# Value rows spread over the partitions, keys written in that order: a block-sparse attention with a gated projection

## The chip, the cores and the metric

The kernel runs on one core of a Trainium2 chip. The metric is the device time of one execution in microseconds, the median of three runs. Engines: TensorE (PE; PEld is its weight load), VectorE (DVE), ScalarE (ACT), GpSimd (POOL) and SyncE (SP), which issues nearly all DMAs.

## The reference

Attention over 4 batches, 8 heads, 768 positions, head size 64. Positions fall into 24 blocks of 32. A query block attends to its own block and both neighbours, to the first and last block, and to three sampled blocks; the first and last query blocks attend to everything. The attention output goes through a gated layer.

```python
mask = np.abs(blk_i - blk_j) <= 1
mask = mask | (blk_i == 0) | (blk_j == 0) | (blk_i == n_blocks - 1) | (blk_j == n_blocks - 1)
for qb in range(n_blocks):
    for kb in sampled_blocks[qb]:
        mask[qb * 32:(qb + 1) * 32, kb * 32:(kb + 1) * 32] = True
scores = np.where(mask, scale * q @ k.T, -1e9)
attn = softmax(scores)                      # rows minus their maximum, exp, divided by the sum
x = (attn @ v)                              # heads side by side: (4, 768, 512)
gate = sigmoid(causal convolution of x with conv_w, 5 taps)
out = (gate * (x @ w_val)) @ w_out
```

## The kernel before

**Places and units.** Batches are taken in two groups of two. Query blocks 1 to 22 form eleven pairs (`PAIRS`); a pair in a group is a *place*, and the list `ORDER` gives their order, with two *global* places (the first and last query block of one batch) put between them, after eight and after nine pairs. A block place gives two *units*, one for each batch of the group; unit 1 and unit 2 of the whole list are exchanged. There are 44 block units.

**One step** of the main loop is: loads for places ahead, `scores` of unit n, key copies for the place ahead, `values` of unit n-2, `transposes` of unit n-1 with up to two pieces of the projection (`fill`, paced by `PACE`) after each half, gate work (`prepare`), and `finish` for the unit whose values are done. Every engine runs its instructions in the program's order (class `InOrder`); the order is fixed when the kernel is built.

**Keys.** `kg` has two buffers, each with 12 slots of one 32-key block: slots 0 to 3 are the first block, the last block and the pair's own two blocks; slots 4 to 7 are the near neighbour and three sampled blocks of the first query block; 8 to 11 the same for the second. Each query block uses slots 0 to 3 and four others, 256 keys. POOL copies them from the resident `keys` (`copy_static`, `copy_sampled`), in the opening partly ACT, and for a few places SP loads the sampled ones from HBM.

**Scores and exponentials.** `scores` fills two PSUM tiles `sc` (heads h = 0, 1) with 32 matmuls; the pool `ps_sc` has three buffers, the third of which the transposed output `xp` takes, so that the next unit's scores use the two tiles that the exponentials read. DVE takes the row maximum of both query blocks (`mx`), and ACT writes four exponentials `pe` of 128 x 256 per unit (two heads, two halves).

**Transposes and values.** PE transposes `pe` in pieces of 128 keys into `pt`, ACT copies them to `ptr`. The key's place among 128 is then its partition, and the values must lie in the same order: `va` holds first, last and own blocks (32 partitions each), `vb` for each query block its near neighbour and three sampled blocks (32 partitions each). The values of a row, two batches with eight heads of 65 numbers, are 4160 bytes.

**Value loads.** `load_values` of a place issues on SP: the end blocks into `va` when the buffer's group changes, the pair's own 64 rows, the near blocks (one DMA for both, or two), a load of six block numbers into registers, and six DMAs of 32 rows each for the sampled blocks. `va` and `vb` have two buffers each; a load waits until PE has used the place before last. For a global place the rows go into 128 partitions.

**The gated layer.** `gates` runs the convolution on DVE with its first tap and tanh on ACT, `split` makes two-part copies of x for exact products (ACT and POOL), `project` does the two products on PE. The weights come as 8-byte integers' worth of double precision and are decoded in the first hundred microseconds: DVE makes `words`, ACT casts to `wv` or `wo`, POOL subtracts for the second part.

Of the kernel before, what the change touches and what calls it, by code (L numbers as in the profile page):

```python
# [11 lines left out]
AF = mybir.ActivationFunctionType  # L12
# [4 lines left out]
B, H, S, D = 4, 8, 768, 64  # L17
BLK, NB, NR = 32, 24, 3
# [47 lines left out]


@with_exitstack
def attention_moe(ctx, tc, qb, kb, v, ve, sampled, w_val, conv_w, w_out, ident_in, slot_in, out):
    nc = tc.nc  # L70
    const = ctx.enter_context(tc.tile_pool(name="const", bufs=1))
    two = ctx.enter_context(tc.tile_pool(name="two", bufs=2))
# [201 lines left out]
    def load_keys(pl):  # L274
        g = pl.gr.g
        if pl.glob:
            return
        pl.kg = kg[pl.kseq % RING]
        if g and pl.p < RING:
            for e in range(EACH):  # L280
                sp.dma_start(pl.kg[:, e, 0:2, :], kb[:, EACH * g + e, 0 : NB : NB - 1, :])
        for place, reg in block_numbers(pl, SP):
            sp.dma_start(
                pl.kg[:, :, place, :],
                kb[:, EACH * g : EACH * g + EACH, bass.ds(reg, 1), :].rearrange("p e o x -> p e (o x)"),
            )
# [8 lines left out]

    def copy_static(pl, e=slice(0, EACH)):
        kt, k, i0 = pl.kg, pl.gr.k, PAIRS[pl.p][0]
        pool.tensor_copy(kt[:, e, 2:4, :], k[:, e, i0 : i0 + 2, :])
        pool.tensor_copy(kt[:, e, 4:9:4, :], k[:, e, i0 - 1 : i0 + 3 : 3, :])
        if pl.p < RING and pl.gr.g == 0:  # L300
            act.copy(kt[:, e, 0:2, :], k[:, e, 0 : NB : NB - 1, :])

    def numbers(pl):
        pl.numbers = {eng: list(block_numbers(pl, eng)) for eng in (POOL, ACT)}
# [15 lines left out]
    def load_values(pl):  # L320
        g = pl.gr.g
        vt = pl.va = va[pl.vseq % VRING]
        pl.vb = two.tile([128, 2, EACH * H * DV], F32, tag="vb", name="vb")
        if pl.glob:
            b = pl.batches[0].b
            x = b % EACH * H * DV
            rows = v[g * S : (g + 1) * S, x : x + H * DV].rearrange("(c p) d -> p c d", p=128)
            vb4 = pl.vb.rearrange("p j (e d) -> p (j e) d", e=EACH)
            for c in range(0, 4, 2):
                sp.dma_start(vb4[:, c : c + 2, :], rows[:, c : c + 2, :])  # L330
            sp.dma_start(vt, rows[:, 4:6, :])
            pl.chunks = [vb4[:, c, :] for c in range(4)] + [vt[:, c, :] for c in range(2)]
            ends.pop(pl.vseq % VRING, None)
            return
        if ends.get(pl.vseq % VRING) != g:
            sp.dma_start(vt[0 : 2 * BLK].rearrange("p e d -> p (e d)"), ve[g])
            ends[pl.vseq % VRING] = g
        i0 = PAIRS[pl.p][0]
        sp.dma_start(
            vt[64:128].rearrange("p e d -> p (e d)"), v[g * S + i0 * BLK : g * S + (i0 + 2) * BLK, :]  # L340
        )
        vblocks = v.rearrange("(n k) d -> n k d", k=BLK)
        if 0 < pl.p < NP - 2:
            sp.dma_start(
                pl.vb[0:BLK], vblocks[g * NB + i0 - 1 : g * NB + i0 + 3 : 3].rearrange("j k d -> k j d")
            )
        else:
            for j, near in enumerate((i0 - 1, i0 + 2)):
                sp.dma_start(pl.vb[0:BLK, j, :], vblocks[g * NB + near if 0 < near < NB - 1 else GROUPS * NB])
        _, regs = nc.values_load_multi_w_load_instructions(  # L350
            sv[0:1, g, i0 : i0 + 2, :].rearrange("p i r -> p (i r)"), engines=[SP], min_val=0, max_val=GROUPS * NB,
            skip_runtime_bounds_check_because="block numbers are drawn from [0, 24)",
        )
        for n, reg in enumerate(regs):
            j, r = n // NR, n % NR
            sp.dma_start(
                pl.vb[BLK * (r + 1) : BLK * (r + 2), j, :], vblocks[bass.ds(reg, 1)].rearrange("o k d -> (o k) d")
            )


# [27 lines left out]
    def scores(un):  # L388
        pr = un.pr
        un.P = []  # L390
        if pr.glob:
            lo = [ps_sc.tile([128, 512], F32, tag="sc", name="s0") for _ in range(2)]
            spaces = ((ps_sc, "sc"), (ps_pt, "pt"))
            hi = [space.tile([128, 512], F32, tag=tag, name="s1") for space, tag in spaces]
            for k0 in range(3):
                for hp, h, rows, cols in heads():
                    dst = hi[h][cols, 0:256] if k0 == 2 else lo[h][cols, 256 * k0 : 256 * k0 + 256]
                    matmul(
                        dst, pr.pl.q[rows, 0, hp, un.e, :], pr.pl.gr.k[rows, pr.i, 8 * k0 : 8 * k0 + 8, cols],
                        start=True, stop=True, tile_position=(64 * h, BLK * hp),  # L400
                    )
            mx = three.tile([128, 2, 4], F32, tag="mx", name="mx")
            rest = five.tile([128, 2, 256], F32, tag="pr", name="rest")
            for h in range(2):
                dve.tensor_reduce(out=mx[:, h, 0:1], in_=lo[h], axis=AX.X, op=ALU.max, negate=True)
                dve.tensor_reduce(out=mx[:, h, 1:2], in_=hi[h][:, 0:256], axis=AX.X, op=ALU.max, negate=True)
                dve.tensor_tensor(out=mx[:, h, 2:3], in0=mx[:, h, 0:1], in1=mx[:, h, 1:2], op=ALU.min)
                first = five.tile([128, 512], F32, tag="pr", name="first")
                act.activation(rest[:, h, :], hi[h][:, 0:256], AF.Exp, bias=mx[:, h, 2:3])
                act.activation(first, lo[h], AF.Exp, bias=mx[:, h, 2:3])  # L410
                un.P.append(first)
            un.P.append(rest.rearrange("p h k -> p (h k)"))
            return
        sc = [ps_sc.tile([128, 2, 256], F32, tag="sc", name="sc") for _ in range(2)]
        kt = pr.pl.kg[:, pr.i].rearrange("p (t e) x -> p t e x", e=4)
        for a in range(2):
            for g in range(4):
                for h in range(2):
                    rows, hp, j = slice(64 * h, 64 * h + 64), 2 * a + g // 2, g % 2
                    matmul(  # L420
                        sc[h][BLK * g : BLK * g + BLK, a, :], pr.pl.q[rows, pr.i, hp, j, :],
                        kt[rows, 0 : 2 + j : 1 + j, :, BLK * hp : BLK * hp + BLK],
                        start=True, stop=True, tile_position=(64 * h, BLK * g),
                    )
        mx = three.tile([128, 2, 4], F32, tag="mx", name="mx")
        for h in range(2):
            dve.tensor_reduce(out=mx[:, h, 0:2], in_=sc[h], axis=AX.X, op=ALU.max, negate=True)
            pe_ = five.tile([128, 2, 256], F32, tag="pr", name="pe")
            for j in range(2):
                act.activation(pe_[:, j, :], sc[h][:, j, :], AF.Exp, bias=mx[:, h, j : j + 1])  # L430
            un.P.append(pe_.rearrange("p j k -> p (j k)"))

    def transposes(un):
# [417 lines left out]
def _layout(inputs):  # L851
    f = np.ascontiguousarray
    k = inputs["k"].reshape(B, HP, 2, NB, BLK, D)
    blocks = np.array([0, NB - 1] + list(range(1, NB - 1)))
    qb = inputs["q"].reshape(B, HP, 2, NB, BLK, D)[:, :, :, blocks].reshape(B, HP, 2, NP, 2, BLK, D)
    qb = f(qb.transpose(2, 6, 0, 3, 1, 4, 5)).reshape(128, B, NP, HP, 2, BLK)
    kb = f(k.transpose(2, 5, 0, 3, 1, 4)).reshape(128, B, NB, HP * BLK)
    vo = np.ones((B, S, H, DV), np.float32)
    vo[..., :D] = inputs["v"].transpose(0, 2, 1, 3)
    vo = vo.reshape(GROUPS, EACH, S, H * DV).transpose(0, 2, 1, 3).reshape(GROUPS * S, EACH * H * DV)  # L860
    vv = np.zeros((GROUPS * S + BLK, EACH * H * DV), np.float32)
    vv[: GROUPS * S] = vo
    ve = f(vo.reshape(GROUPS, NB, BLK, -1)[:, 0 : NB : NB - 1]).reshape(GROUPS, 2 * BLK, EACH * H * DV)
    w_val = f(inputs["moe_w_val"]).view(np.int64)
    w_out = f(inputs["moe_w_out"]).view(np.int64)
    conv = f(inputs["moe_conv_w"].T.reshape(CH, 128, KW).transpose(1, 0, 2)).reshape(128, CH * KW).view(np.int64)
    ident = np.eye(128, dtype=np.float32)
    slot = np.arange(NB, dtype=np.float32)[None]
    return {
        "q": qb, "k": kb, "v": vv, "ve": ve, "sampled": f(np.asarray(inputs["sampled_blocks"], np.int64)),  # L870
        "w_val": w_val, "conv_w": conv, "w_out": w_out, "ident": ident, "slot": slot,
    }

# [20 lines left out]
```

## Time and profile before

| | |
|---|---|
| median of three runs | 393.9 us (393.18 to 394.4) |
| the profiled execution's own time | 396.17 us |
| its span, first to last instruction | 394.4 us |
| PE busy | 345.2 us, 88% |
| DVE busy | 247.0 us, 63% |
| ACT busy | 245.3 us, 62% |
| POOL busy | 155.1 us, 39% |
| DMA, the main queue | 64.03 MB, 58.7% of 16 engines' span |
| mean granted TensorE clock | 0.967 of full |

The shares are averages over stages with different limits: an engine that is busy for 62% of the span can be the bound in one stage and idle in the next. Matmuls are pipelined, so a busy PE is not PE at its peak.

### The profile page before, as it was taken

What the parts mean: (1) busy time and instruction counts of PE and PEld (TensorE: products, weight loads), DVE (VectorE), ACT (ScalarE), POOL (GpSimd) and SP (SyncE); (2) the same over time, 40 slices, a digit from 0 to 9 for tenths busy, and PEclk for the clock granted to TensorE, in tenths of its full rate; (3) what the DMA queues carried; (4) which work ended last, traced back from release to release, by engine and by line L of the source; (5) the groups of instructions that cost most, each with busy time, mean ns of one, the idle gap of its engine ahead of it and who ended that gap; (6) DMA issues with size and microseconds to landing.
All of it is one profiled execution on the core that took longest, in us unless ns stands there. A gap on an engine that the chain in (4) does not pass through costs nothing.

```text
span 394.4 us, 15210 instructions
## 1 busy us (share of the span) xinstructions
PE 345.2 (88%) x6240; PEld 270.1 (68%) x6240; DVE 247.0 (63%) x534; ACT 245.3 (62%) x574; POOL 155.1 (39%) x233
## 2 busy tenths in 40 slices
PE   0589878786999999988899999998999899998985
PEld 0256555564787688856698777866769668887874
DVE  3333777777877873463964895459845665285940
ACT  2665767767678885573766876577746755364531
POOL 1452256647328011325643970327303720344440
PEclk9968999998999999996999999999999989999999
DMA  7996899997625676899865578454345241010202
GB/s 257 282 232 187 238 237 262 264 222 203 179 48 137 238 236 184 265 246 279 233 192 134 129 193 220 103 183 118 109 158 138 64 130 54 2 54 27 75 6 80
DMA packets 34568, 65.08 MB, mean 165 GB/s; under 512 B 4931, under 2 KB 18372, under 8 KB 34500
## 3 DMA queue, kind: packets, MB, share of 16 engines
q1 hardware_dynamic: 34210, 64.03, 58.7%
q8 instruction: 49, 0.80, 0.9%
q14 instruction: 19, 0.16, 0.1%
q10 hardware_dynamic: 290, 0.09, 0.1%
HBM read 57.81 MB, written 6.29 MB: 163 GB/s over the span
## 4 chain that ended last, share of the span: by engine, by line
PE 52%; DVE 17%; issue 9%; DMA 6%; POOL 6%; ACT 4%; SPq 3%; POOLq 1%; ACTq 0%; DVEq 0%
PE vp L87 15%; DVE th L87 10%; PE av L87 9%; PE op L87 9%; PE pt L87 8%; PE sc L87 7%; DVE mx L87 5%; POOL kg L87 4%; DMA vb<-in_v 4%; SPq L87 2%; PE s L87 2%; PE xp L87 2%; DMA keys<-in_k 2%; ACT pe L87 1%; POOLq L251 1%
## 5 line engine op out<-in xcount | busy, mean ns | idle before, releaser
L87 DVE SCALAR_TENSOR_TENSOR th<-xT,cw,th 128x388 f32<-128x388 f32 (+1 forms) x128 | 94.0, 748 | 12.3 <-ACT th L87 9.7
L87 ACT ACTIVATE pe<-sc,mx 128x256 f32<-128x256 f32 x176 | 68.9, 475 | 47.9 <-DVE mx L87 47.8
L87 DVE TENSOR_REDUCE mx<-sc 128x2 f32<-128x512 f32 x88 | 56.5, 683 | 66.5 <-PE sc L87 66.0
L87 POOL COPY kg<-keys 128x256 f32 (+3 forms) x156 | 76.0, 530 | 53.6 <-DMA keys<-in_k 28.1
L87 ACT COPY ptr<-pt 128x512 f32<-128x512 f32 x112 | 64.9, 599 | 25.9 <-PE pt L87 25.7
L87 POOL TENSOR_TENSOR yl<-y,yh 128x384 fp32r<-128x384 f32 x32 | 33.5, 1048 | 118.4 <-ACT yh L87 118.1
L87 PE MATMUL sc<-kg,qc 64*32 64x256 f32 x1408 | 54.7, 397 | 18.3 <-ACT kg L87 10.2
L87 PE MATMUL av<-vb,ptr 128*32 128x65 f32 x1920 | 51.4, 228 | 8.0 <-DMA vb<-in_v 7.6
L87 PE MATMUL pt<-ident,pe 128*128 128x128 f32 x352 | 54.2, 289 | 3.6 <-ACT rest L87 2.1
L87 PE MATMUL vp<-xh,wv 128*128 128x384 f32 (+1 forms) x256 | 52.3, 346 | 3.1 <-DVE y L87 3.1
L87 PE MATMUL op<-wo,yh 128*128 128x512 f32 x192 | 54.1, 404 | 0.0
L87 PEld LDWEIGHTS av<-va,ptr 128*32 128x32 f32 (+1 forms) x1312 | 36.7, 121 | 19.6 <-issue 9.5
L87 PEld LDWEIGHTS av<-vb,ptr 128*32 128x32 f32 x1920 | 40.5, 114 | 13.8 <-issue 8.5
L87 PEld LDWEIGHTS pt<-ident,pe 128*128 128x128 f32 x352 | 40.8, 146 | 11.1 <-issue 3.1
L87 PE MATMUL av<-va,ptr 128*32 128x65 f32 (+1 forms) x1312 | 47.7, 231 | 0.5 <-ACT ptr L87 0.5
L87 PEld LDWEIGHTS sc<-kg,qc 64*32 64x32 f32 x1408 | 23.1, 109 | 36.0 <-POOL kg L87 16.1
L87 PEld LDWEIGHTS vp<-xh,wv 128*128 128x128 f32 x256 | 43.8, 188 | 4.1 <-issue 3.7
L87 POOL TENSOR_TENSOR xl<-xT,xh 128x384 fp32r<-128x384 f32 (+1 forms) x32 | 36.1, 1137 | 24.3 <-ACT xh L87 19.7
L87 PEld LDWEIGHTS op<-wo,yh 128*128 128x128 f32 x192 | 35.2, 190 | 7.0
L87 PE MATMUL op<-wo,yl 128*128 128x512 f32 x96 | 32.8, 423 | 2.4 <-POOL yl L87 2.3
L87 DVE SCALAR_TENSOR_TENSOR y<-th,vp 128x384 f32<-128x384 f32 (+2 forms) x48 | 18.6, 414 | 20.1 <-PE vp L87 18.9
L87 PE MATMUL vp<-xl,wv 128*128 128x388 f32 (+1 forms) x128 | 27.8, 338 | 0.0
(63 smaller groups left out, 360.2 us busy)
## 6 DMA issues: line engine op xcount, KB each, us to landing
vb<-in_v SPq DMA_DIRECT2D x140, 130.0 KB, 4.1
keys<-in_k SPq DMA_DIRECT2D x12, 512.0 KB, 5.1
va<-in_v SPq DMA_DIRECT2D x22, 260.0 KB, 4.6
qc<-in_q SPq DMA_DIRECT2D x20, 256.0 KB, 3.5
out<-ot SPq DMA_DIRECT2D x20, 256.0 KB, 2.0
vb<-in_v SPq DMA_DIRECT2D x18, 260.0 KB, 5.9
vb<-in_v SPq DMA_DIRECT2D x8, 520.0 KB, 4.9
kg<-in_k SPq DMA_DIRECT2D x28, 128.0 KB, 3.2
```

Of the source, the lines that this page charges most:

```text
L87: made = getattr(self.eng, name)(*args, **kwargs)
L251: _, regs = nc.values_load_multi_w_load_instructions(sm[0:1, first : first + len(mine)], engines=[eng], min_val=0, max_val=NB - 1, skip_ru ...
```

## The change

The 32 rows of a value block no longer fill 32 neighbouring partitions. In `va` the end blocks take the even partitions and the own blocks the odd ones, row k of the four blocks at partitions 4k to 4k+3; in `vb` the near block and the three sampled blocks do the same, each at every fourth partition. The host lays the end blocks out row by row for that, and passes the own pairs once more in an array `vp` with the two blocks' rows interleaved. Slots 1 and 2 of `kg` change places (first, own, last, own), so the own keys are written in two pieces. The exponentials read their 256 scores as before and write key k of slot s at position 4k+s of its 128, so neighbouring keys land four elements, 16 bytes, apart. The transposes and the value matmuls stay as they are.

```diff
-            sp.dma_start(vt[0 : 2 * BLK].rearrange("p e d -> p (e d)"), ve[g])
+            sp.dma_start(vt[0:128:2].rearrange("p e d -> p (e d)"), ve[g])
         i0 = PAIRS[pl.p][0]
         sp.dma_start(
-            vt[64:128].rearrange("p e d -> p (e d)"), v[g * S + i0 * BLK : g * S + (i0 + 2) * BLK, :]
+            vt[1:128:2].rearrange("p e d -> p (e d)"), vp[g, pl.p]
         )
...
-                pl.vb[0:BLK], vblocks[g * NB + i0 - 1 : g * NB + i0 + 3 : 3].rearrange("j k d -> k j d")
+                pl.vb[0:128:4], vblocks[g * NB + i0 - 1 : g * NB + i0 + 3 : 3].rearrange("j k d -> k j d")
...
-                pl.vb[BLK * (r + 1) : BLK * (r + 2), j, :], vblocks[bass.ds(reg, 1)].rearrange("o k d -> (o k) d")
+                pl.vb[r + 1 : 128 : 4, j, :], vblocks[bass.ds(reg, 1)].rearrange("o k d -> (o k) d")
...
-        pool.tensor_copy(kt[:, e, 2:4, :], k[:, e, i0 : i0 + 2, :])
+        pool.tensor_copy(kt[:, e, 1:4:2, :], k[:, e, i0 : i0 + 2, :])
...
-                act.activation(pe_[:, j, :], sc[h][:, j, :], AF.Exp, bias=mx[:, h, j : j + 1])
+                act.activation(
+                    pe_[:, j, :].rearrange("p (t k s) -> p t s k", t=2, s=4),
+                    sc[h][:, j, :].rearrange("p (t s k) -> p t s k", t=2, s=4), AF.Exp, bias=mx[:, h, j : j + 1],
+                )
```

The copies and loads of the end keys into slots 0 and 2 change in the same way. No instruction is added, removed or moved: all five engines have the same instructions in the same order, with other access patterns.

## Rows read from the trace of the kernel before

**Rows 1.** Busy time of each engine in stretches of the span: stretch in us, its length, then busy us and number of instructions for PE, PEld, DVE, ACT and POOL, the granted TensorE clock, the busy share of the DMA engines, and GB/s.
```profile
40.00:60.00 20.00, 16.32 (x364) 11.19 (x363) 14.68 (x35) 14.35 (x35) 7.34 (x11) 1.00 0.96 237
...
200.00:220.00 20.00, 20.00 (x374) 16.80 (x373) 9.81 (x27) 13.55 (x34) 9.23 (x14) 1.00 0.55 145
340.00:360.00 20.00, 18.47 (x93) 16.25 (x92) 14.73 (x23) 9.56 (x20) 8.73 (x9) 1.00 0.11 40
```

**Rows 2.** The DMA engines from 80 to 100 us in 40 slices of 0.5 us: mean busy share in tenths, and GB/s moved.
```profile
DMA  9999999999999999995995376886116594999999
GB/s 250 224 225 191 235 155 196 234 215 145 218 241 208 241 233 233 250 258 123 192 267 127 114 204 180 229 236 176 38 41 191 171 204 150 395 408 383 404 379 366
```

**Rows 3.** DMA issues of the sampled value blocks: count, size of one, median us from issue to landing.
```profile
vb<-in_v SPq DMA_DIRECT2D x140, 130.0 KB, 4.1
```

**Rows 4.** All instructions on the tile `vb`: idle time of the engine that ended with a landed value block (us, times), and us from issue to landing of all its loads.
```profile
  DMA vb<-in_v: 11.5, 9
...
DMA to landing us min/median/max: 2.5/4.2/6.8
```

**Rows 5.** Instructions of PE in order of time, value matmuls that waited for a value block: start us, length us, engine, operation, operands, shape, count, and in brackets the idle time before them.
```profile
30.43 0.84 PE L87 MATMUL av<-vb,ptr 128*32 128x65 f32 x28 [1.62 <-DMA vb<-in_v]
...
44.76 0.66 PE L87 MATMUL av<-vb,ptr 128*32 128x65 f32 x30 [1.28 <-DMA vb<-in_v]
...
55.28 0.66 PE L87 MATMUL av<-vb,ptr 128*32 128x65 f32 x30 [1.34 <-DMA vb<-in_v]
...
178.89 0.29 PE L87 MATMUL av<-vb,ptr 128*32 128x65 f32 x1 [1.62 <-DMA vb<-in_v]
```

**Rows 6.** The chain of work that ended last, two of its pieces: start us, length us, what (the transfer from its issue to its landing).
```profile
25.25 5.09 DMA vb<-in_v
...
175.50 3.15 DMA vb<-in_v
```

**Rows 7.** SP's issues in order of time, the seven `vb` DMAs of two places: start, time from the first to the last issue's end.
```profile
36.17 5.89 SPq L87 DMA_DIRECT2D vb<-in_v  x7
...
82.69 4.72 SPq L87 DMA_DIRECT2D vb<-in_v  x7
```

**Rows 8.** Groups of ACT instructions: operands, output and input shape, count, busy us, mean ns of one, idle us before them.
```profile
L87 ACT ACTIVATE pe<-sc,mx 128x256 f32<-128x256 f32 x176 | 68.9, 475 | 47.9 <-DVE mx L87 47.8
L87 ACT COPY ptr<-pt 128x512 f32<-128x512 f32 x112 | 64.9, 599 | 25.9 <-PE pt L87 25.7
...
L87 ACT COPY xT<-xp 128x256 f32<-128x256 f32 x44 | 17.1, 388 | 8.0 <-PE xp L87 7.8
```

**Rows 9.** Groups of DVE instructions on the 72 block numbers, same columns. `tmp<-sf` reads and writes neighbouring elements; `sm<-sb` reads at a step of 8 bytes, `sf<-sb` at 24; `sv<-tmp` writes at 12.
```profile
L87 DVE TENSOR_SCALAR tmp<-sf 1x72 f32<-1x72 f32 x3 | 0.5, 179 | 0.0
L87 DVE TENSOR_SCALAR sv<-tmp 1x72 int32<-1x72 f32 x2 | 0.5, 238 | 0.1
...
L87 DVE CAST sf<-sb 1x72 f32<-1x72 int32 x1 | 0.3, 261 | 0.0
...
L87 DVE COPY sm<-sb 1x72 int32<-1x72 int32 x1 | 0.2, 185 | 1.3 <-DMA sb<-in_sampled 1.3
```

**Rows 10.** Busy time in steps of one unit, each from the first score matmul of a unit to that of the next; columns as in rows 1. Four such steps are this short before 100 us; the first two and the last are shown.
```profile
33.60:37.52 3.92, 3.87 (x91) 2.63 (x90) 1.96 (x5) 2.91 (x8) 0.00 (x0) 0.94 0.17 24
37.52:41.32 3.80, 3.67 (x92) 2.60 (x91) 2.45 (x7) 2.81 (x8) 1.09 (x3) 1.00 0.83 222
...
87.13:91.09 3.96, 3.84 (x92) 2.82 (x91) 3.86 (x11) 3.24 (x9) 1.81 (x1) 1.00 0.87 205
```

**Rows 11.** ACT and PE in order of time in the second of these steps: the four exponentials, and the score matmuls of the next unit.
```profile
39.53 1.57 ACT L87 ACTIVATE pe<-sc,mx 128x256 f32<-128x256 f32 x4 [0.99 <-DVE mx L87]
...
41.32 1.11 PE L87 MATMUL sc<-kg,qc 64*32 64x256 f32 x32
```

**Rows 12.** The opening, in order of time: weight loads of the second unit's scores, and ACT's copies of keys for the third.
```profile
14.90 0.61 PEld L87 LDWEIGHTS sc<-kg,qc 64*32 64x32 f32 x30 [2.56 <-ACT pe L87]
...
18.54 1.01 ACT L87 COPY kg<-keys 128x256 f32<-128x256 f32 x4
```

**Rows 13.** ACT, POOL and PE in order of time from 65 to 73 us.
```profile
65.54 1.57 ACT L87 ACTIVATE pe<-sc,mx 128x256 f32<-128x256 f32 x4 [2.77 <-DVE mx L87]
...
67.49 0.63 ACT L87 CAST wv<-words 128x512 fp32r<-128x512 f32 x1
...
68.19 1.27 POOL L87 TENSOR_TENSOR wv<-words,wv 128x512 fp32r<-128x512 f32 x1 [3.56 <-ACT wv L87]
...
72.63 1.09 PE L87 MATMUL sc<-kg,qc 64*32 64x256 f32 x32
```

**Rows 14.** PE at the first global unit, scores that waited for ACT's copy of the transposed output.
```profile
95.40 1.07 PE L87 MATMUL s<-keys,qg 64*32 64x256 f32 x16 [3.09 <-ACT xT L87]
```

**Rows 15.** The chain of work that ended last, its pieces on exponentials after 200 us.
```profile
216.21 0.89 ACT pe L87 x3
...
277.83 0.83 ACT pe L87 x2
...
303.78 1.25 ACT pe L87 x4
```

**Rows 16.** ACT in order of time in the step that begins at 149.72, with the idle time before its exponentials and before the copy of the second half.
```profile
151.63 1.57 ACT L87 ACTIVATE pe<-sc,mx 128x256 f32<-128x256 f32 x4 [1.27 <-DVE mx L87]
...
155.24 0.59 ACT L87 COPY ptr<-pt 128x512 f32<-128x512 f32 x1 [1.16 <-PE pt L87]
```

More of the change, by code (lines that the diff above doesn't have):

```diff
@@ L68, in attention_moe @@
 @with_exitstack
-def attention_moe(ctx, tc, qb, kb, v, ve, sampled, w_val, conv_w, w_out, ident_in, slot_in, out):
+def attention_moe(ctx, tc, qb, kb, v, ve, vp, sampled, w_val, conv_w, w_out, ident_in, slot_in, out):
     nc = tc.nc
@@ L280, in load_keys @@
             for e in range(EACH):
-                sp.dma_start(pl.kg[:, e, 0:2, :], kb[:, EACH * g + e, 0 : NB : NB - 1, :])
+                sp.dma_start(pl.kg[:, e, 0:4:2, :], kb[:, EACH * g + e, 0 : NB : NB - 1, :])
         for place, reg in block_numbers(pl, SP):
@@ L297, in copy_static @@
         kt, k, i0 = pl.kg, pl.gr.k, PAIRS[pl.p][0]
-        pool.tensor_copy(kt[:, e, 2:4, :], k[:, e, i0 : i0 + 2, :])
+        pool.tensor_copy(kt[:, e, 1:4:2, :], k[:, e, i0 : i0 + 2, :])
         pool.tensor_copy(kt[:, e, 4:9:4, :], k[:, e, i0 - 1 : i0 + 3 : 3, :])
         if pl.p < RING and pl.gr.g == 0:
-            act.copy(kt[:, e, 0:2, :], k[:, e, 0 : NB : NB - 1, :])
+            act.copy(kt[:, e, 0:4:2, :], k[:, e, 0 : NB : NB - 1, :])
     def numbers(pl):
@@ L348, in load_values @@
             for j, near in enumerate((i0 - 1, i0 + 2)):
-                sp.dma_start(pl.vb[0:BLK, j, :], vblocks[g * NB + near if 0 < near < NB - 1 else GROUPS * NB])
+                sp.dma_start(pl.vb[0:128:4, j, :], vblocks[g * NB + near if 0 < near < NB - 1 else GROUPS * NB])
         _, regs = nc.values_load_multi_w_load_instructions(
@@ L862, in _layout @@
     vv[: GROUPS * S] = vo
-    ve = f(vo.reshape(GROUPS, NB, BLK, -1)[:, 0 : NB : NB - 1]).reshape(GROUPS, 2 * BLK, EACH * H * DV)
+    by_block = vo.reshape(GROUPS, NB, BLK, EACH * H * DV)
+    ve = f(by_block[:, 0 : NB : NB - 1].transpose(0, 2, 1, 3)).reshape(GROUPS, 2 * BLK, EACH * H * DV)
+    vp = by_block[:, 1 : NB - 1].reshape(GROUPS, NP - 1, 2, BLK, EACH * H * DV)
+    vp = f(vp.transpose(0, 1, 3, 2, 4)).reshape(GROUPS, NP - 1, 2 * BLK, EACH * H * DV)
     w_val = f(inputs["moe_w_val"]).view(np.int64)
@@ L869, in _layout @@
     return {
-        "q": qb, "k": kb, "v": vv, "ve": ve, "sampled": f(np.asarray(inputs["sampled_blocks"], np.int64)),
+        "q": qb, "k": kb, "v": vv, "ve": ve, "vp": vp, "sampled": f(np.asarray(inputs["sampled_blocks"], np.int64)),
         "w_val": w_val, "conv_w": conv, "w_out": w_out, "ident": ident, "slot": slot,
```

## The prediction

> **What bounds the kernel now.** I read the busy times by stretch first [rows 1]. Three stages show. Between 40 and 60 us PE is busy for 16.32 of 20 us while the DMA engines are busy 0.96 of the time: this stage has little DMA room. Between 200 and 220 us PE is busy for all of its 20 us and ScalarE (ACT) for 13.55: PE sets the time. After 340 us the DMA share is 0.11, and neither value loads nor exponentials of block units are left. The change can thus act in the first 100 us, at single stalls after it, and not in the tail.
>
> Then the rate of the transfers [rows 2]. From 80 to 90 us, where the queue holds value blocks for 32 partitions, the DMA engines are fully busy and move 123 to 258 GB/s, most of the time above 190. From 97 to 100 us they are as busy and move 366 to 408 GB/s: there the queue holds the 520 KB loads of a global unit, from the same array of values, but into 128 partitions. Busy engines with half the bytes say that something behind the engines is narrow for the 32-row transfers, and the partitions they land in are what differs. The Trainium skill has the rule for it (SBUF — State Buffer, section "Door 1: The DMA port swizzle"): 32 contiguous partitions reach 8 of 16 ports, and so do 64; a set that takes every fourth partition reaches all by its bit formula. By that rule, the trace agrees on the two levels; no run here shows the stepped set yet.
>
> Then who waits for values [rows 4]: PE sat idle 11.5 us in 9 waits that ended with a value block, and a block takes 2.5 us at least, 4.2 in the median and 6.8 at most to land.
>
> **What the change removes.** A block transfer is 130 KB [rows 3]. At about 225 GB/s it holds the engines for 0.59 us, at about 390 for 0.34. The order of instructions is the same on every engine; so are the number of DMAs and the time SP needs to issue them. What can go are the waits, one by one:
>
> - 30.43 us: 1.62 us of idle PE [rows 5]. The block that ended it was issued at 25.25 and took 5.09 us [rows 6]. With a shorter queue it lands in about 3 us, before PE comes to it. Gain 1.6.
> - 44.76 us: 1.28 us [rows 5]. SP took 5.89 us for the seven issues of this place, and 4.72 for the same seven in a place where it was held less [rows 7]. The difference, 1.2 us, is the gain.
> - 55.28 us: 1.34 us [rows 5], behind a weight transfer, queries and two places of values. Gain 1.3.
> - 178.89 us: 1.62 us [rows 5]. Its last block was issued at 175.50 and landed 3.15 us later [rows 6]; the shortest landing is 2.5 [rows 4]. Only 0.65 can go, since SP issues too late.
>
> Together 4.8 us. The lower bound of this term is zero (if the stepped rows are no faster).
>
> **What the change adds.** 176 exponentials of 128x256 now write with a step of four elements, 16 bytes; each takes 475 ns now [rows 8]. No ACT instruction before writes with such a step, so I bound its price. From below: nothing, if ACT writes one element per cycle wherever it lands. From above, by VectorE: three small instructions on 72 elements [rows 9]. A copy that reads at a step of 8 bytes takes 185 ns, a plain one on contiguous elements 179; the conversion of the same words read at 24 bytes takes 261, and the one that writes at 12 bytes takes 238. So 8 bytes cost nothing, 24 bytes cost (261-185)/72 = 1.06 ns per element, one more cycle of that engine, and a write at 12 bytes 0.8 ns. These are reads and writes of SBUF at steps on both sides of 16 bytes, so they are the nearest rows. I take one more ACT cycle per element: from 128x512 to 128x256 its copies fall from 599 to 388 ns [rows 8], 0.82 ns per element, thus 256 x 0.82 = 0.21 us per exponential, 0.84 for the four of a unit, 37 us of ACT busy in all. The bounds are 0 and 0.27 us.
>
> The Trainium skill has a rule that speaks against this change (SBUF — State Buffer, section "Specifications (TRN2)"): a cacheline of SBUF is 16 bytes and an access pattern needs two hits in a line for full bandwidth. A step of four floats never has two. The VectorE rows agree; for ACT no run here shows it. By the rule the sum comes out at the +2.7 us below, without it at the -4.8 of the first rival.
>
> Where is that 0.84 us on the path?
>
> - Opening. The score matmuls of the second unit at 14.90 waited 2.56 us for the first exponentials [rows 12]: two exponentials, 0.42. The key copies of ACT at 18.54, for which the third unit's matmuls wait, stand behind the second unit's four: 0.84. Cost 1.3.
> - Short units. At four places before 100 us the step from one unit's scores to the next takes only 3.80 to 3.96 us, with PE busy nearly throughout [rows 10]. There the loop scores, maximum, exponentials, next scores (which reuse the PSUM tiles the exponentials read) is nearly as short: exponentials start at 39.53 and take 1.57, to 41.10; the next scores start at 41.32 [rows 11]. With 0.84 more they end at 41.94 and PE waits until about 42.0. Four times about 0.65: cost 2.6.
> - Key copies of POOL. At 65.54 four exponentials run, behind them ACT converts a weight (67.49), behind it POOL subtracts (68.19), and behind that it copies the keys for which the scores at 72.63 wait [rows 13]. This chain is tight: cost 0.84. In the neighbouring places it has about as much slack as the delay.
> - The global unit at 95.40, which waited 3.09 us for an ACT copy [rows 14] behind a group of exponentials: cost 0.84.
> - After 200 us the chain that ended last runs through nine exponentials, at 216.21, 277.83 and 303.78 [rows 15]: 9 x 0.21 = 1.9.
>
> Together 7.5 us. Elsewhere after 100 us the delay is covered by PE's projection matmuls: in the step at 149.72 ACT stands idle for 1.27 us before its exponentials and 1.16 later [rows 16], more than 0.84. Without that cover each of the 28 units after the first global one (44 block units, which are 176 exponentials by four, less the 16 of the first eight places) would cost up to 0.84. POOL's copy of own keys in two runs of 128 instead of one of 256 is costed at nothing: the copy of the neighbours' keys beside it already has that form, and POOL is busy for 7.34 us of 20 [rows 1].
>
> **The sum.** 7.5 - 4.8 = +2.7 us on the profiled execution, 396.17 to 398.9. That execution lies 2.3 us above the median of the runs shown, 393.9; on the median the same sum gives 396.6.
>
> **The rivals.**
>
> (1) ACT writes at a step as fast as without. Then only the gain is left: 393.9 - 4.8 = 389.1, faster. For it: no row shows ACT slow at a step. Against it: the VectorE rows. It decides from the price per exponential: the 7.5 us scale with 0.21, so below about 0.13 us each the change gains. Another page of the Trainium skill (ScalarE: Activation LUTs, section "What ACT_TABLE_LOAD costs") gives an activation a time by its length alone and so stands for this rival.
>
> (2) The stepped rows land no faster: the change does not do what it says, because two DMA engines still meet at one port when each carries two rows. Then 393.9 + 7.5 = 401.4. Against it: 128-partition loads run at the high level [rows 2]; for it: how 32 stepped rows are dealt to the engines is seen nowhere.
>
> (3) Neither acts: 393.9, no change.
>
> **How the numbers follow.** I give ACT's price a chance of 0.72, since reads and writes on another engine both show it, and the faster landing 0.8. The forecast (both) then has 0.58, rival 1 0.22, rival 2 0.14, rival 3 0.06. The likeliest case's own range is 394 to 401: with the four short units hidden the costs are 4.9 and the sum is nothing; with the upper price they are 9.6, and three more exposed units add 2.5. The range for all goes from 388.5, just under rival 1, to 402.5, rival 2 and a little; worse (all 16 units of the first eight places exposed: 13.4 + 1.9 - 4.8 = +10.5) is left out. A difference under 0.3%, 1.2 us, can't be told from none. Within the forecast I give slower 0.65, same 0.22, faster 0.13, since its sum lies only 1.5 us beyond that bound; rival 1 is nearly all faster (0.20), rival 2 slower, rival 3 the same. Slower 0.52, same 0.20, faster 0.28.
>
> **What would show it.** The mean of an exponential: 0.69 us if right, 0.475 for rival 1. Landing of a block: median near 3 us against 4.2, and a DMA share of 40 to 60 us near 0.7; unchanged for rival 2. PE's idle time that ends with a value block: under 4 us instead of 11.5. New waits of the score matmuls for exponentials in the units before 90 us, steps of 4.5 instead of 3.8 us. I am wrong if ACT is slowed and yet no step grows (the PSUM loop was not tight), or if value loads that land sooner let weights, queries and keys behind them come sooner, which I have counted at nothing.

## The result, and the profile after

The changed kernel takes 398.54 us in the median of 14 runs, the kernel before 396.0 in 14 runs beside it: ratio 1.0115, with an interval of 1.0083 to 1.0147. Two later comparisons gave 1.0074 [1.0019, 1.0128] and 1.0037 [0.9998, 1.0077]. So it is slower, by 0.4 to 1.2%, though the third interval just reaches 1. The ratios leave out disturbed runs, so they need not equal the quotient of two medians: over all runs these are 398.54 and 396.0, 395.95 and 396.73, 398.26 and 395.64 us, in the second comparison the other way round. Most runs of one kernel lie within 1% of their median, and the profiled execution of the changed kernel is one of its shortest (395.76 us; that of before is 396.17). The two profiles can thus not show the difference as a whole; they are compared stage by stage.

The page of the changed kernel: busy time, the main DMA queue, the exponentials and the block loads, which answer to [rows 3, 8]; below it, from the order of time, the four exponentials of one unit.

```profile
PE 348.4 (88%) x6240; PEld 269.0 (68%) x6240; DVE 247.1 (63%) x534; ACT 268.2 (68%) x574; POOL 153.2 (39%) x233
...
q1 hardware_dynamic: 34210, 64.03, 52.1%
...
L87 ACT ACTIVATE pe<-sc,mx 128x256 f32<-128x256 f32 x176 | 95.5, 712 | 41.6 <-DVE mx L87 41.4
...
vb<-in_v SPq DMA_DIRECT2D x140, 130.0 KB, 3.1
```

```profile
213.69 2.17 ACT L87 ACTIVATE pe<-sc,mx 128x256 f32<-128x256 f32 x4 [0.69 <-DVE mx L87]
```

ACT is busy for 23 us more. An exponential takes 712 ns instead of 475, but the four of a unit overlap: together they take 2.17 us instead of 1.57 [rows 11, 16], 0.60 more, not four times 237 ns. A block lands in 3.1 us instead of 4.1, and the same bytes hold the DMA engines for 52.1% of the span, not 58.7%. Both things that the forecast was made of happen. The tile `vb` of the changed kernel, to be read beside [rows 4]; in the first line the ns SP spends on an issue, least, median and most:

```profile
L87 SPq DMA_DIRECT2D vb<-in_v x166: 368/484/1926, 9.0 to 319.3; - x166
...
  DMA vb<-in_v: 9.2, 5
...
DMA to landing us min/median/max: 2.4/3.1/6.1
```

The same first line of the kernel before:

```profile
L87 SPq DMA_DIRECT2D vb<-in_v x166: 315/325/1722, 9.5 to 318.6; - x166
```

This is what the forecast missed. A block into every fourth partition keeps SP for 484 ns, a block into 32 neighbouring ones for 325. Blocks land sooner after their issue, but SP issues fewer in the same time, and the idle time of PE that ends with a value block falls only from 11.5 to 9.2 us. These two figures count the waits of the weight loader beside those of the matmuls; for the matmuls alone the view of waits (who waits for whom, us, times, longest) has, before and after:

```profile
PE av L87 <- DMA vb<-in_v: 7.6, 6, 1.6
PE av L87 <- DMA vb<-in_v: 6.1, 3, 2.6
```

The changed kernel in two stretches, columns and stretches as in [rows 1]:

```profile
40.00:60.00 20.00, 16.94 (x358) 11.03 (x358) 14.23 (x32) 15.95 (x33) 11.98 (x19) 1.00 0.79 241
...
200.00:220.00 20.00, 19.70 (x426) 15.50 (x428) 10.47 (x25) 14.61 (x32) 10.77 (x16) 1.00 0.43 123
```

Between 40 and 60 us the DMA engines move 241 GB/s (237 before) while busy for 0.79 of the time (0.96): there is room now. From 75 to 95 us of the changed kernel, in slices of 0.5 us, to be read beside [rows 2]:

```profile
DMA  0278599896437745587787605760177779479999
GB/s 8 58 225 191 181 277 308 333 200 208 167 74 216 133 150 133 167 233 208 167 207 238 232 23 135 219 173 12 55 225 202 219 194 214 82 283 395 387 412 412
```

The seven issues of one place run from 77.42 to 83.84. From the eleventh slice on, 80 to 83.5 us, the engines are busy for 0.3 to 0.7 and move 74 to 216 GB/s: in the mean of the 16 engines nothing is full, the queue waits for SP. Before, the loads of this place kept the engines at 0.9 and above. Of the 6.42 us SP spends 3.97 on the seven issues themselves (the sum of their lengths in the trace), before 2.27 of 4.72: the 1.70 us between the two are theirs. The bound went from the transfer to the issue. SP's `vb` issues in order of time, first the same two places as in [rows 7], then the eight issues of the place for which PE waits near 174 us:

```profile
31.61 6.52 SPq L87 DMA_DIRECT2D vb<-in_v  x7
...
77.42 6.42 SPq L87 DMA_DIRECT2D vb<-in_v  x7
...
167.45 6.49 SPq L87 DMA_DIRECT2D vb<-in_v  x8
```

And that last place in the kernel before:

```profile
170.47 5.35 SPq L87 DMA_DIRECT2D vb<-in_v  x8
```

PE's stalls on value blocks in the changed kernel, to be read beside [rows 5]:

```profile
41.19 0.66 PE L87 MATMUL av<-vb,ptr 128*32 128x65 f32 x30 [1.70 <-DMA vb<-in_v]
...
173.90 0.43 PE L87 MATMUL av<-vb,ptr 128*32 128x65 f32 x2 [2.57 <-DMA vb<-in_v]
...
176.15 0.29 PE L87 MATMUL av<-vb,ptr 128*32 128x65 f32 x1 [1.83 <-DMA vb<-in_v]
```

The stalls of 30.43 and 55.28 are gone. That of 44.76 stands, 1.70 us long instead of 1.28. The two at the end belong to one place and grew: 2.57 and 1.83 us, where before there were 1.62 at 178.89 [rows 5] and, at 176.98,

```profile
176.98 0.30 PE L87 MATMUL av<-vb,ptr 128*32 128x65 f32 x2 [1.52 <-DMA vb<-in_v]
```

The other half, the waits for exponentials; this is the view of waits of the changed kernel (who waits for whom, us, times, longest):

```profile
PEld sc L87 <- ACT pe L87: 6.2, 12, 2.9
```

and its line of the kernel before:

```profile
PEld sc L87 <- ACT pe L87: 3.4, 6, 2.6
```

Score matmuls wait for exponentials twice as often. Where, is seen in the steps (columns as in [rows 10]). The first two and the last of the short steps of the changed kernel, then four steps after 190 us:

```profile
28.80:32.92 4.12, 4.10 (x91) 2.73 (x90) 1.96 (x5) 3.88 (x9) 1.34 (x4) 1.00 0.76 237
32.92:37.11 4.19, 4.08 (x91) 2.73 (x90) 2.43 (x7) 3.34 (x8) 1.09 (x3) 1.00 0.58 187
81.65:86.04 4.39, 4.31 (x91) 2.81 (x90) 4.06 (x11) 4.22 (x11) 1.28 (x1) 1.00 0.71 189
...
192.70:200.80 8.10, 8.10 (x131) 6.89 (x130) 5.16 (x13) 6.43 (x14) 2.23 (x5) 1.00 0.69 196
211.80:218.50 6.70, 6.40 (x122) 4.62 (x121) 3.70 (x9) 6.01 (x14) 5.36 (x8) 1.00 0.45 126
228.60:235.40 6.80, 6.80 (x127) 4.95 (x130) 6.54 (x14) 6.50 (x14) 4.30 (x8) 1.00 0.62 194
239.10:244.90 5.80, 5.80 (x119) 4.71 (x118) 2.16 (x6) 4.91 (x12) 0.00 (x0) 1.00 0.69 209
```

The same four late steps in the kernel before:

```profile
195.70:203.40 7.70, 7.70 (x137) 6.79 (x136) 5.40 (x13) 5.44 (x13) 2.55 (x5) 1.00 0.65 178
214.30:220.50 6.20, 6.20 (x124) 4.67 (x124) 3.73 (x9) 5.51 (x14) 4.97 (x8) 1.00 0.58 144
230.60:236.80 6.20, 6.20 (x123) 4.78 (x123) 5.99 (x13) 5.38 (x13) 4.22 (x8) 1.00 0.63 170
240.50:245.90 5.40, 5.40 (x119) 4.61 (x118) 2.18 (x7) 3.95 (x11) 0.00 (x0) 1.00 0.68 208
```

(The bounds are rounded to 0.1 us; from first score matmul to first score matmul the four grow by 0.53, 0.54, 0.55 and 0.42 us.) A busy PE hides the wait: its rows are busy for the whole step, but the score matmuls are drawn out. The weight loads of the third of these steps in the changed kernel:

```profile
228.62 0.13 PEld L87 LDWEIGHTS sc<-kg,qc 64*32 64x32 f32 x2 [0.17 <-issue]
229.05 0.61 PEld L87 LDWEIGHTS sc<-kg,qc 64*32 64x32 f32 x30 [0.29 <-ACT pe L87]
```

and before:

```profile
230.60 0.61 PEld L87 LDWEIGHTS sc<-kg,qc 64*32 64x32 f32 x32 [0.17 <-ACT pe L87]
```

The first two loads find their PSUM tile free; the other thirty wait for the last exponentials of the unit before, which end late now. Before, the exponentials were already what released these loads, but without delay: the 0.17 us stand just as well where nothing was waited for. So the loop of [rows 11] was closed here with next to no slack. The first and the fourth step read the same, before and after. In the second the output product waits for POOL's `yl`, whose source ACT writes behind its exponentials: 0.74 us instead of 0.20.

### The profile page after: what moved, and what is told of

Read it like the earlier page. It is cut to its first block, busy times and chain, and to the rows that moved or that the text cites. A ratio compares the mean times of both kernels' runs of the same rounds, so it can differ in the third digit from the quotient of the medians.

```text
span 394.0 us, 15210 instructions
## 1 busy us (share of the span) xinstructions
PE 348.4 (88%) x6240; PEld 269.0 (68%) x6240; DVE 247.1 (63%) x534; ACT 268.2 (68%) x574; POOL 153.2 (39%) x233
## 3 DMA queue, kind: packets, MB, share of 16 engines
q1 hardware_dynamic: 34210, 64.03, 52.1%
## 4 chain that ended last, share of the span: by engine, by line
PE 55%; DVE 18%; issue 9%; ACT 6%; POOL 6%; DMA 2%; SPq 1%; POOLq 1%; ACTq 0%; DVEq 0%
PE vp L87 15%; DVE th L87 10%; PE sc L87 10%; PE op L87 9%; PE av L87 9%; PE pt L87 8%; DVE mx L87 6%; POOL kg L87 4%; ACT pe L87 3%; PE s L87 2%; PE xp L87 2%; DMA qc<-in_q 1%; SPq L87 1%; POOLq L251 1%; ACT th L87 1%
## 5 line engine op out<-in xcount | busy, mean ns | idle before, releaser
L87 ACT ACTIVATE pe<-sc,mx 128x256 f32<-128x256 f32 x176 | 95.5, 712 | 41.6 <-DVE mx L87 41.4
L87 DVE SCALAR_TENSOR_TENSOR th<-xT,cw,th 128x388 f32<-128x388 f32 (+1 forms) x128 | 93.4, 744 | 14.0 <-ACT th L87 11.5
L87 POOL COPY kg<-keys 128x256 f32 (+3 forms) x156 | 74.9, 525 | 50.6 <-DMA keys<-in_k 27.3
L87 ACT COPY ptr<-pt 128x512 f32<-128x512 f32 x112 | 67.8, 625 | 15.8 <-PE pt L87 15.7
L87 PE MATMUL sc<-kg,qc 64*32 64x256 f32 x1408 | 59.4, 396 | 17.9 <-ACT kg L87 9.7
L87 PE MATMUL av<-vb,ptr 128*32 128x65 f32 x1920 | 50.4, 227 | 6.1 <-DMA vb<-in_v 6.1
L87 PE MATMUL pt<-ident,pe 128*128 128x128 f32 x352 | 53.2, 285 | 2.5 <-ACT rest L87 2.3
L87 PEld LDWEIGHTS sc<-kg,qc 64*32 64x32 f32 x1408 | 24.6, 108 | 38.4 <-POOL kg L87 16.1
L87 PEld LDWEIGHTS av<-vb,ptr 128*32 128x32 f32 x1920 | 39.7, 113 | 11.5 <-issue 6.8
L87 PEld LDWEIGHTS pt<-ident,pe 128*128 128x128 f32 x352 | 39.7, 144 | 9.9 <-ACT rest L87 3.2
```

The lines of the kernel that those rows point to most:

```text
L87: made = getattr(self.eng, name)(*args, **kwargs)
```

## The experiments

**The two halves apart.** First the changed kernel with the old exponentials:

```diff
-                act.activation(
-                    pe_[:, j, :].rearrange("p (t k s) -> p t s k", t=2, s=4),
-                    sc[h][:, j, :].rearrange("p (t s k) -> p t s k", t=2, s=4), AF.Exp, bias=mx[:, h, j : j + 1],
-                )
+                act.activation(pe_[:, j, :], sc[h][:, j, :], AF.Exp, bias=mx[:, h, j : j + 1])
```

> The value rows spread as in the changed kernel, the exponentials written without a step as before (keys and values are then in different orders, so the product of the two is another one; the work is the same). My theory, gain and cost add: faster than before by 4.8 us, ratio 0.988 (0.982 to 0.994); exponentials at 475 ns, landing of a 32-row block near 3.1 us, PE's idle time that ends with a value block under 4 us. Rival, the waits for values only hide other waits (key copies, the next issue of SP): ratio 0.997 to 1.003, with the same short landing.

Measured: 394.56 us, ratio to before 0.9955 [0.9921, 0.9989]. The faster loads alone gain 1.8 us, not 4.8. An exponential takes 477 ns here, so nothing but the step makes it 712. POOL's key copies, the own keys now in two pieces, cost nothing: the largest group takes 497 ns each in the changed kernel, 505 before. The same kernel again, because the difference is small:

> The value rows spread, exponentials without a step (keys and values are then in different orders; the work is the same), once more. Ratio 0.992 to 0.998, about 2 us faster than before; steps after 200 us as in the kernel before.

394.59 us, 0.9964 [0.9927, 1.0001]. The reverse is the kernel before with the stepped write alone, the diff above turned round:

> The kernel before with the exponentials written at a step of four elements; values, loads and key slots as before (keys and values are then in different orders; the work is the same). My theory: slower than before by 7.5 us scaled to the 712 ns measured, 8.5 us, ratio 1.021 (1.015 to 1.028). Rival, most of the delay is covered and the changed kernel is slower for another reason (the spread loads or the split key copies cost): ratio below 1.006.

397.15 us, 1.0040 [1.0005, 1.0076]; an exponential takes 712 ns. And again:

> The kernel before with the exponentials written at a step of four elements, once more (keys and values are then in different orders; the work is the same). Both theories: 1.003 to 1.007. Its second profile should show the same longer steps after 200 us as the first (2.6 us in five steps), and a first 100 us that is no longer than before by more than 2 us.

397.72 us, 1.0044 [1.0001, 1.0087]. The stepped write costs 1.7 us, not 7.5. Both terms of the forecast had the right sign and were too large.

**Where the loads lose their gain.** SP's eight `vb` issues before 174 us and the two steps in which PE waits for them, in the kernel with the stepped loads alone:

```profile
169.19 7.24 SPq L87 DMA_DIRECT2D vb<-in_v  x8
```

```profile
172.75:190.30 17.55, 13.57 (x232) 10.41 (x232) 9.07 (x19) 8.87 (x22) 8.40 (x14) 0.81 0.82 267
```

and in the kernel with the stepped exponentials alone:

```profile
171.82 5.36 SPq L87 DMA_DIRECT2D vb<-in_v  x8
```

```profile
175.65:192.50 16.85, 12.08 (x232) 8.73 (x231) 11.55 (x21) 11.40 (x25) 6.13 (x9) 1.00 0.90 246
```

Counted from the first score matmul of the step, SP ends the place's issues 1.5 us later with contiguous rows (171.82 + 5.36 - 175.65) and 3.7 us later with stepped ones (169.19 + 7.24 - 172.75). These two steps take 17.33 to 18.69 us in the seven profiles with stepped loads and the old order of scores, and 14.64 to 17.14 us in the six with contiguous loads. Not all of that is the loads: the granted clock takes part. Its mean over the two steps (1 is 2.4 GHz, and it falls to 1.2) is 0.80 to 0.82 in all seven with stepped loads; with contiguous ones it is 0.80 in two, before and in the second profile of the exponentials alone (17.14 us), and 0.89 to 1.00 in the other four. The kernel before:

```profile
174.12:191.14 17.02, 13.88 (x231) 10.60 (x230) 9.11 (x19) 8.83 (x22) 9.82 (x16) 0.80 1.01 276
```

So the kind of load alone doesn't set the clock. Between profiles of like clock the means, 17.86 and 17.08, are 0.8 us apart: that much of what they save early the stepped loads lose here. Whether the longer stay at the low clock is chance or follows from the later values isn't shown.

**Where the exponentials cost.** The kernel before with the stepped write in the first eight places only, then from the ninth on:

```diff
+                dst, src_ = pe_[:, j, :], sc[h][:, j, :]
+                if un.pl.vseq < 8:          # in the second kernel: >= 8
+                    dst = dst.rearrange("p (t k s) -> p t s k", t=2, s=4)
+                    src_ = src_.rearrange("p (t s k) -> p t s k", t=2, s=4)
+                act.activation(dst, src_, AF.Exp, bias=mx[:, h, j : j + 1])
```

> The kernel before with the stepped exponentials in the first eight places only, the 16 units of the first 100 us (there keys and values are in different orders; the work is the same). The prediction's terms for that stretch: 1.3 + 2.6 + 0.84 + 0.84 = 5.6 us at 0.21 us each, 6.3 us at the measured 0.237: ratio 1.016. Rival, the delay is hidden there behind the waits for values, key copies and weights that the stage has anyway, and shows only after 200 us: ratio 0.997 to 1.003.

394.93 us, 0.9982 [0.9942, 1.0023]: nothing to be seen of the 5.6 us that I had put there.

> The kernel before with the stepped exponentials from the ninth place on only, the 28 units after the first 90 us (there keys and values are in different orders; the work is the same). If the whole price falls there, as the longer steps of the profiles say: ratio 1.003 to 1.008, 2 us, and no step before 100 us changes. The prediction's terms for this stretch: 1.9 us at 0.21 us each, 2.1 at 0.237, thus 1.005.

397.95 us, 1.0052 [1.0012, 1.0092]: 2.1 us, the whole cost. The third and fourth of the late steps in the kernel with stepped exponentials alone:

```profile
233.70:240.41 6.71, 6.71 (x123) 4.90 (x122) 6.49 (x14) 6.44 (x14) 4.30 (x8) 1.00 0.59 170
244.10:249.98 5.88, 5.88 (x121) 4.77 (x121) 2.19 (x7) 5.00 (x12) 0.00 (x0) 1.00 0.62 189
```

and in the one with stepped loads alone:

```profile
229.66:235.83 6.17, 6.17 (x119) 4.75 (x118) 5.96 (x13) 5.39 (x13) 4.24 (x8) 1.00 0.71 219
239.53:245.00 5.47, 5.47 (x119) 4.63 (x118) 2.21 (x7) 4.03 (x11) 0.00 (x0) 1.00 0.74 240
```

The four steps have the longer length in every profile with the stepped write in these units and the shorter one where it is contiguous, to 0.04 us, but for one (8.01 us for the first step, with the write stepped in the first eight places); the version below with stepped score matmuls is left aside. Their growth adds up to 2.0 us, and both kernels that carry it without stepped loads are slower by about that. A fifth step grows too, the one with the exponentials of 277.83 [rows 15], here before and after:

```profile
273.95:279.77 5.82, 5.59 (x147) 4.19 (x146) 5.71 (x10) 4.61 (x12) 5.29 (x9) 1.00 0.46 128
272.94:279.33 6.39, 5.60 (x147) 4.19 (x147) 6.25 (x11) 5.18 (x12) 5.34 (x9) 1.00 0.48 137
```

PE's second transposes wait 0.79 us there for ACT's copy behind the exponentials, 0.23 before. The step takes 5.82 to 5.84 us in four profiles with the contiguous write and 6.38 to 6.40 in four with the stepped one, all at the full clock; in four more, where the clock fell in the step before, it takes 5.37 and 5.38 contiguous, 5.48 and 5.53 stepped.

**What a step costs ACT.** The kernel before, with exponentials at a step of 1, 2, 4 and 8 elements by turns of places; the tiles are named `pea` to `ped` to keep them apart:

```diff
+            step_ = (1, 2, 4, 8)[un.pl.vseq % 4]
...
+                    pe_[:, j, :].rearrange("p (k s) -> p s k", s=step_),
+                    sc[h][:, j, :].rearrange("p (s k) -> p s k", s=step_), AF.Exp, bias=mx[:, h, j : j + 1],
```

> The kernel before with the exponentials of every fourth place written at a step of 1, 2, 4 and 8 elements (tiles pea, peb, pec, ped; keys and values are then in different orders; the work is the same). If what costs is a new 16-byte line for every element: 475, 475, 712 and 712 ns. If any step costs: 712 at 2 already. If it grows with the step: more than 712 at 8.

```profile
L87 ACT ACTIVATE ped<-sc,mx 128x256 f32<-128x256 f32 x40 | 22.2, 726 | 7.0 <-DVE mx L87 6.9
L87 ACT ACTIVATE pec<-sc,mx 128x256 f32<-128x256 f32 x40 | 21.7, 710 | 8.0 <-DVE mx L87 7.9
L87 ACT ACTIVATE peb<-sc,mx 128x256 f32<-128x256 f32 x48 | 19.2, 492 | 15.2 <-DVE mx L87 15.2
L87 ACT ACTIVATE pea<-sc,mx 128x256 f32<-128x256 f32 x48 | 18.8, 476 | 13.0 <-DVE mx L87 13.0
```

A step of 8 bytes costs 16 ns in 256 elements, 16 bytes 234, 32 bytes 250: one threshold between 8 and 16, and flat on both sides. Beyond it the price is 0.92 ns per element (236/256 with the 712 of the changed kernel). The rule of the Trainium skill (SBUF — State Buffer, section "Specifications (TRN2)"), two hits in a 16-byte line for full bandwidth, agrees with these four rows. The other page of the Trainium skill that I had named (ScalarE: Activation LUTs, section "What ACT_TABLE_LOAD costs"), which gives such an activation a time by its length alone, does not: 256 elements take 476 or 712 ns.

**The order made elsewhere.** If a stepped write is dear, the keys can be put in order where it may be cheap. In the first version the score matmuls read the keys of the four slots in turn, 512 bytes apart, and the exponentials are the old ones:

```diff
-                        kt[rows, 0 : 2 + j : 1 + j, :, BLK * hp : BLK * hp + BLK],
+                        kt[rows, 0 : 2 + j : 1 + j, :, BLK * hp : BLK * hp + BLK].rearrange("p t e x -> p t x e"),
```

> The changed kernel's loads, but the score matmuls read their keys in the interleaved order (512 bytes apart), so that the exponentials read and write without a step. If a step costs PE nothing, since a four-byte matmul column takes several passes: score matmuls at 0.376 us as before and ratio 0.988. If it costs PE one more column time or more: score matmuls near 0.5 us or longer, and at 1408 of them in groups of four some 10 to 45 us more: ratio 1.01 to 1.10.

414.22 us, 1.0482 [1.0439, 1.0525]:

```profile
L87 PE MATMUL sc<-kg,qc 64*32 64x256 f32 x1408 | 94.7, 628 | 14.0 <-ACT kg L87 9.6
```

A score matmul takes 628 ns where 397 stood: PE pays 40 us more for reading at a distance, and 18 us of it reach the end. In the second version ACT reads the scores from PSUM in the new order and writes neighbours, the same pairs of element and place as in the changed kernel:

```diff
-                    pe_[:, j, :].rearrange("p (t k s) -> p t s k", t=2, s=4),
-                    sc[h][:, j, :].rearrange("p (t s k) -> p t s k", t=2, s=4), AF.Exp, bias=mx[:, h, j : j + 1],
+                    pe_[:, j, :].rearrange("p (t k s) -> p t k s", t=2, s=4),
+                    sc[h][:, j, :].rearrange("p (t s k) -> p t k s", t=2, s=4), AF.Exp, bias=mx[:, h, j : j + 1],
```

> The changed kernel, but the exponentials read the scores in PSUM in the stepped order (32 elements apart) and write neighbouring elements. If only writes to SBUF at a step are dear: exponentials at 475 ns and the gain of the loads alone, ratio to before 0.988. If a step costs on either side: exponentials near 700 ns and the changed kernel's own ratio, 1.01.

```profile
L87 ACT ACTIVATE pe<-sc,mx 128x256 f32<-128x256 f32 x176 | 69.1, 477 | 51.6 <-DVE mx L87 51.6
```

393.52 us, 0.9985 [0.9943, 1.0027]. The jump of 128 bytes between reads of PSUM costs nothing that can be seen (477 ns against 475). The same kernel again, beside the changed kernel again:

> The changed kernel with the step on the reading side, in PSUM, once more: it holds the gain of the loads without the price of the exponentials. Ratio 0.990 to 0.996; faster than the changed kernel by 2.6 us (the five longer steps after 200 us gone) to 5 us.

393.86 us, 0.9934 [0.9897, 0.9972].

> The changed kernel once more, beside its parts on one chip. If the parts add (loads alone -1.5 us, exponentials alone +1.1 us in the medians so far): ratio to before 0.997 to 1.003, and the 1.0115 of the first comparison was largely chance of the runs. If the two together cost more than apart: again 1.008 to 1.015, and slower than the kernel with the exponentials alone.

395.95 us, 1.0074 [1.0019, 1.0128]. A third comparison of the changed kernel:

> The changed kernel a third time, beside one of its parts. If the parts add: 0.997 to 1.003. If they cost more together than apart: 1.007 to 1.012.

398.26 us, 1.0037 [0.9998, 1.0077]. The version that reads at a step puts every exponential where the changed kernel puts it, and has the stepped loads without the longer exponentials. It is faster than the changed kernel (393.86 against 395.95 us in the same comparison) and, by 0.4% in the mean of its two ratios, than the one before; of their two intervals the first includes 1.

## Why the prediction was right, and where its sum was wrong

The forecast was slower, 396.6 us against 393.9, a ratio of 1.007; three comparisons gave 1.0115, 1.0074 and 1.0037. (The three runs behind the 393.9 lie 2.1 us under the median of 14, so only the ratios can be compared.) Both mechanisms act: blocks land sooner, and longer exponentials hold up the next scores. Their sizes were wrong: the gain of 4.8 us measured 1.4 to 1.8, the cost of 7.5 measured 1.6 to 2.1. By the measured parts the sum would have been about nothing, so that the whole lies so near the forecast is in part luck.

- **Landing and DMA share: right.** Median 3.1 us (near 3 said), share between 40 and 60 us 0.79 (near 0.7 said). Rival 2 is out. In [rows 2] the 123 GB/s that I counted among the busy slices belongs to one with a share of 0.5; the busy ones move 145 to 258.
- **Price of an exponential: right for one, wrong for a unit.** 0.71 us (0.69 said). Rival 1, 0.475, is out, and the VectorE rows were the better guide [rows 9]. But "0.84 for the four of a unit" adds up four exponentials that overlap: the four end 0.60 us later, 2.17 instead of 1.57, and ACT is busy for 23 us more, not 37. [rows 11] had the overlap: 1.57 us for the four, where four times 475 ns make 1.90. Scaled by 0.60/0.84, the 7.5 us would have been 5.4.
- **The gain: 4.8 said, 1.4 to 1.8 measured (stepped loads alone).** The step that failed is "so are the number of DMAs and the time SP needs to issue them". An issue went from 325 to 484 ns. The stalls of the matmuls behind a full queue (30.43, 55.28) are gone in the changed kernel; in the two profiles of the loads alone the weight loader still waits 0.92 us at the first in one, the matmuls 0.32 at the second, and nothing is left in the other. That of 44.76 is 1.70 us in the changed kernel, and 0.69 and nothing with the loads alone. I had read SP's 5.89 us for seven issues as 4.72 plus holding by a full queue, and they now take 6.4 to 6.5 in either place. The 0.65 at 178.89 turned into a loss: that line of the forecast said "since SP issues too late", and SP now issues later. Value waits of 9.2 us, where under 4 was said, show the same. With the loads alone the matmuls' waits for values fall from 7.6 us to 5.0 and 3.7, by more than the time does; what takes up the rest stays open. The "11.5 us in 9 waits" was a misreading as well: three of the nine are the weight loader's, two of them the same stalls again.
- **The early cost: 5.6 said, none measured.** What failed is that each wait was added to the total. The three short steps shown are 4.12, 4.19 and 4.39 us long, 0.20 to 0.43 more, where steps of 4.5 were said; the fourth, at 46.78, stays at 3.85. (A fifth, at 72.63, takes 3.71 and was overlooked.) The step of the first global unit grows from 9.05 to 9.99 us in the profiles of before and after (0.84 said), but the granted clock of the two differs:

```profile
91.09:100.14 9.05, 5.96 (x108) 3.94 (x107) 6.67 (x14) 7.17 (x17) 8.21 (x11) 0.81 0.77 240
86.04:96.03 9.99, 6.16 (x107) 4.11 (x106) 7.66 (x15) 7.89 (x19) 8.86 (x12) 0.78 0.74 232
89.57:99.29 9.72, 6.12 (x108) 4.07 (x107) 7.65 (x16) 7.64 (x18) 8.87 (x12) 0.77 0.76 228
```

The third row is the second profile of the version that reads PSUM at a step, with no stepped write: at its clock the step grows by 0.3 us only. With the stepped exponentials in the first eight places alone it takes 9.31 at 0.82, and that kernel's total shows none of it. Why the stage as a whole swallows the delay is argued, not shown: PE waits there for keys, weights and values in turn, and what one wait adds, the next one may lose. The opening and the key copies can't be told apart from the scatter of their steps between profiles.

- **The late cost: 1.9 said, about 2.1 measured, but in part in other places.** I read it off the chain that ended last, as nine exponentials at 216.21, 277.83 and 303.78 [rows 15]; the chain has three more beside these, one at 217.29 and two at 277.09, all four of each unit. The steps with 216.21 and 277.83 grow, by 0.54 and 0.57 in the two profiles. The one with 303.78 stays at 7.48 us. Three steps that grow, near 196, 231 and 240 us, have no exponential on that chain. The claim that failed is "Elsewhere after 100 us the delay is covered". It was drawn from one step, at 149.72 [rows 16], which indeed stays at 5.58 us. In two of the late steps ACT was already busy for 5.4 to 5.5 of 6.2 us, and in three the next unit's scores were released by its exponentials with next to no slack. That the size came out right is luck.
- **The sum of the parts.** Loads alone -0.4%, exponentials alone +0.4%: together they should be no change, rival 3's time by another way. The three ratios of the whole are all above 1. The changed kernel also lies 2.1 to 5.0 us above the version that reads PSUM at a step, medians of the same or neighbouring comparisons, though it differs from it by ACT's time alone; the five late steps account for 2.1 to 2.6 of that and the first global step for 0.3 at like clock. Whether the rest is the two parts acting on each other or the scatter between comparisons stays open.

## What to carry to other kernels

Spreading the rows of a small DMA over the partitions sped up its landing here (4.1 to 3.1 us), but each issue cost SP more (325 to 484 ns): read the time of the issue before counting on the gain, since a queue bound by the DMA engines can become one bound by SP. The permutation was best put on the side of ACT that reads PSUM, where it cost nothing; the write side paid from a step of 16 bytes on, and so did the matmuls' moving operand at 512 bytes, in eight times as many instructions. Price a group of instructions that overlap from its first start to its last end, not by the mean of one times their number. And the chain that ended last names one path only; whether a longer instruction is covered is asked step by step, by ACT's busy share in the step and by what the next unit's first matmul waits for. Compare two steps only at the same granted clock.

## What the runs showed of the hardware

- SP's issue of a block load (140 of the 166 are 130 KB) takes 325 ns into 32 neighbouring partitions and 484 ns into every fourth one, in the median.
- An exponential of 128 x 256 from PSUM takes 476, 492, 710 and 726 ns with a write step of 4, 8, 16 and 32 bytes, and 477 ns with a read step of 128 bytes in PSUM. Four of them in a row take 1.57 us with neighbouring writes and 2.17 with a step of 16 bytes.
- A matmul of 64 x 256 whose moving operand jumps 512 bytes from element to element takes 628 ns instead of 397.
- Between 40 and 60 us, where value blocks go into every fourth partition, 241 GB/s keep the DMA engines busy for 0.79 of the time; with 32 neighbouring partitions 237 GB/s took 0.96. The Trainium skill's port rule (SBUF — State Buffer, section "Door 1: The DMA port swizzle") agrees with the direction; how the rows are dealt to the engines was not seen.
